# A causal convolution on TensorE: windows of 128 rows and 122 tokens against tiles of 64 rows and 58 tokens in the quarters of the array

## The chip, the cores and the metric

The kernel runs on one NeuronCore of one Trainium2 chip. The core has five engines with an instruction stream each: TensorE (PE in the profile; its weight loads are PEld), VectorE (DVE), ScalarE (ACT), GpSimd (POOL) and SyncE (SP, which here only issues DMAs). TensorE reads SBUF and writes PSUM; PSUM has eight banks of 512 float32 columns on 128 partitions. The metric is the device time of one execution in microseconds, the median over several runs. Each program is also profiled once; the profile gives the span from the first to the last instruction, start and duration of each instruction, and what ended the idle time before it.

## The reference, cut to what matters

```python
# x (8, 4224, 192); weight (8 heads, 7); moe_w_val, moe_w_out (192, 192); moe_conv_w (5, 192)
w = softmax(weight, axis=-1)                       # 7 taps for each of 8 heads
x_pad = concat([zeros(B, 6, D), x], axis=1)
x = sum_k w[h, k] * x_pad[:, s + k, h * 24 : h * 24 + 24]      # 24 channels to a head
gate_pre = sum_k conv_w[k] * pad(x, 4)[:, k : k + S, :]        # 5 taps, one weight per channel
gate = 1 / (1 + exp(-gate_pre))
out = (gate * (x @ w_val)) @ w_out
```

The first convolution has the same seven weights for all 24 channels of a head. The second has five weights per channel. Between them and the output lie two products with 192x192 matrices. All is float32.

## The kernel before, in words

**Tokens.** The eight sequences are laid end to end in two streams of four, so that each step handles two streams at once. Tokens are cut into 14 groups; `NJS` gives a group's size n (2, 3 or 5), and a group is cut into two or three steps by `BLOCKS` (304 and 302, twice 448, three times 502 tokens; the last group 500 and 188). There are 36 steps.

**First convolution (`conv_unit`, L304).** It runs on TensorE as a product with a band matrix. A window has 128 token rows (`WK`) and gives 122 tokens (`WIN`). For head h and window j the stationary operand is the input, 128 token rows by 120 columns (24 channels x 5 pieces of the group); the moving operand is `band`, 128 rows by 122 columns, which holds the softmaxed taps. The result lies channels by tokens. A unit is four windows in one PSUM bank, copied by ScalarE into `e` (L327); after a head's last window its rows go by DMA from `e` to the step layouts x1 and x2 (`scatter`, L339). The 192 channels are kept as 128 in x1 (both streams side by side, chunk a, index 0) and 64 + 64 in x2 (both streams stacked on partitions, chunk b, index 1).

**Second convolution.** It runs on ScalarE and VectorE. `gate_open` writes tap 0 into a PSUM accumulator (pa for chunk a, two banks; pb for chunk b, one bank), `gate_taps` adds taps 1 to 4 on VectorE (L397), `gate_close` takes the sigmoid on ScalarE (L410).

**Products.** Float32 values are split into a rounded float32r part h (cast on ScalarE, L418 and L426) and a rest l (subtraction on GpSimd, L419 and L427), and three products w.h*h + w.l*h + w.h*l are summed. v is the product with w_val, o the one with w_out. The 192x192 matrix is cut into blocks: `main` (128x128), `rows` (two row halves of 64), `diagonal` (128x128 with two blocks of 64), and `columns`, which stays in float32, cut into four pieces of the tokens and two column halves of the array. `gated` (L510) multiplies v by the sigmoid on VectorE, `split_gated1` and `split_gated2` split the result, `project` (L526) copies o out of PSUM and sends it.

**PSUM.** pa takes two banks, pb one; the other five are the pool `ps`, from which each of the six accumulators of a step (v2, v0, v1, o2, o0, o1; L433) and each unit of the convolution takes one bank.

**Order.** All engines run in the order in which the program is written (`manual_schedule`). Step n works on v of step n and o of step n-1; the convolution in it makes units of a group two groups ahead (`todo`, L547). Steps 0 to 3 are written out in a loop of their own (L580). From step 4 on the loop at L643 runs; there the taps of later steps are placed by `ahead`, `LEAD`, `BETWEEN`, `COST` and `FITS`: as many as a table of leads asks for, in the order all four of chunk a, all four of chunk b. `flush` closes a chunk whose taps are done and opens that chunk of the next step. On ScalarE, `flush(1)` stands behind `split_gated1` and in front of `project(n - 1, 0)`.

Of the kernel before, what the change touches and what calls it, by code (L numbers as in the profile page):

```python
# [7 lines left out]
F32 = mybir.dt.float32  # L8
# [10 lines left out]
HALO = KG - 1  # L19
WIN = 122  # L20
WK = WIN + KW - 1
NS = 5
# [7 lines left out]


NJS = [2, 3, 3, 3] + [5] * 8 + [3, 3]


def half(n):
    return (n * WIN - (KW - 1 if n % 2 else 0)) // 2


def reach(n):
    return 2 * n * WIN + half(n)  # L40
# [12 lines left out]


BLOCKS = {2: (304, 302), 3: (448, 448), 5: (502, 502, 502)}
for _n, _b in BLOCKS.items():
    assert sum(_b) == room(_n)
LEFT = TOTAL - sum(sum(BLOCKS[n]) for n in NJS[:-1])
# [17 lines left out]
LAST = N - 1  # L76
MB = 502
NMAX = max(NJS)
# [29 lines left out]
def kernel(  # L108
# [62 lines left out]
    w0 = cp.tile([128, NH, KW], F32, name="w0")  # L171
    band = cp.tile([WK, NH, WIN], F32, name="band")
    halves = [slice(4 * q, 4 * q + 4) for q in range(2)]
# [27 lines left out]
    nc.vector.memset(one, 1.0)  # L201
    zero = cp.tile([WK, M + WIN], F32, name="zero")
    nc.vector.memset(zero, 0.0)
# [3 lines left out]
    def zeros(k):  # L207
        pw = ps.tile([128, 512], F32, tag="p", name="pw")
        for i in range(k):
            nc.tensor.matmul(pw[:M, :WIN], lhsT=zero[:, :M], rhs=zero[:, M:], start=True, stop=True)  # L210
# [23 lines left out]
    for q in halves:  # L234
        nc.vector.tensor_tensor(out=band[:, q], in0=band[:, q], in1=wide(rs, WIN, q), op=ALU.mult)
    warm2 = cp.tile([128, 1], F32, name="warm2")
# [56 lines left out]


    x1s, x2s, es = {}, {}, {}
    units = []
    for g, n in enumerate(NJS):
        for q in range(2):
            ws = [(hi, j) for hi in range(4) for j in range(n)]
            for i in range(0, len(ws), 4):  # L300
                units.append((g, q, ws[i : i + 4]))
    first_unit = [next(i for i, u in enumerate(units) if u[0] == g) for g in range(NG)] + [len(units)]

    def conv_unit(u):  # L304
        g, q, ws = units[u]
        n = NJS[g]
        if u == first_unit[g]:
            x1s[g] = xp.tile([128, 2 * XB], F32, tag="x1", name=f"x1_{g}")
            x2s[g] = xp.tile([128, XC], F32, tag="x2", name=f"x2_{g}")
        if ws[0] == (0, 0):  # L310
            es[g, q] = ep.tile([M, 4 * NMAX * WIN], F32, tag="e", name=f"e_{g}_{q}")
        e = es[g, q]
        pc = ps.tile([128, 512], F32, tag="p", name=f"pc_{u}")
        for k, (hi, j) in enumerate(ws):
            h = QUADS[q][hi]
            i, at = home[g, h]
            c = (at * n + j) * M
            nc.tensor.matmul(  # L318
                pc[:M, k * WIN : (k + 1) * WIN],
                lhsT=xtiles[i][:, c : c + M],  # L320
                rhs=band[:, 4 * q + hi, :],
                start=True,
                stop=True,
            )
        a = (ws[0][0] * n + ws[0][1]) * WIN
        w = len(ws) * WIN
        nc.scalar.copy(e[:, a : a + w], pc[:M, :w])  # L327
# [64 lines left out]
    def gate_taps(n, i, k0=1, k1=KG):  # L392
        if n >= N:
            return
        acc = accs[n, i]
        for k in range(k0, k1):
            nc.vector.scalar_tensor_tensor(  # L397
                out=acc, in0=views(n, k)[i], scalar=cwt[:, i, k : k + 1],
                in1=acc, op0=ALU.mult, op1=ALU.add,
            )  # L400
# [21 lines left out]
    def split2(pool, tag, n, x):  # L422
# [5 lines left out]
        return h, l  # L428

    HALVES = (slice(0, 64), slice(64, 128))  # L430

# [14 lines left out]
    def diagonal(what, n):  # L446
        if not ok(n):
            return
        acc = bank(what, n, 2)
        w, _, _, h2, l2 = operands(what, n)  # L450
        r = slice(W22, W22 + 128)
        for i, (a, b) in enumerate(parts(w, h2, l2)):
            nc.tensor.matmul(acc, lhsT=a[:, r], rhs=b, start=(i == 0), stop=False)  # L453
# [26 lines left out]
    def columns(what, n):  # L480
        if not ok(n):
            return
        m = STEPS[n][2]
        acc = banks[what, n, 2]
        w = w_val if what == "v" else w_out
        x = views(n)[0] if what == "v" else g1s[n]
        cuts = [m * i // 4 for i in range(5)]
        for i in range(4):
            c = slice(cuts[i], cuts[i + 1])
            for q, p in enumerate(HALVES):  # L490
                nc.tensor.matmul(  # L491
                    acc[p, c], lhsT=w.f[:, W12 : W12 + 64], rhs=x[:, q, c],
                    start=False, stop=(i == 3),
                )
# [46 lines left out]
    def conv(k):  # L541
        for _ in range(k):
            if done[0] < len(units):
                conv_unit(done[0])
                done[0] += 1

    todo = [0] * (N + 1)  # L547
    for g in range(LAG, NG):
        a, b = SOON.get(g) or (first[g - LAG], first[g - 1])
        if g == NG - 1:  # L550
            a, b = a - 1, b - 1
        k = first_unit[g + 1] - first_unit[g]
        for i in range(k):
            todo[a + i * (b - a) // k] += 1
# [9 lines left out]
    zeros(WARM[1])  # L564
    conv(3)
    w_out.cast(nc.vector)
# [53 lines left out]
    T = KG - 1  # L620
    taps = [(n, i, k) for n in range(HEAD + 1, N) for i in range(2) for k in range(1, KG)]
    at_tap = [0]
    pending = []

    def flush(*which):
        for n, i in [p for p in pending if p[1] in which]:
            gate_close(n, i)
            gate_open(n + 1, i)
            pending.remove((n, i))

    def tap():
        n, i, k = taps[at_tap[0]]
        at_tap[0] += 1
        flush(*(j for m, j in pending if m < n and j == i))
        gate_taps(n, i, k, k + 1)
        if k == T:
            pending.append((n, i))

    def ahead(n):
        lead = LEAD[max(k for k in LEAD if k <= n)]  # L640
        return min(2 * T * (n - HEAD) + T + lead, len(taps))

    for n in range(HEAD, N + 1):  # L643
        diagonal("v", n)
        split(n + 1)
        diagonal("o", n - 1)
        main("v", n, 0)
        main("v", n, 1)
        while at_tap[0] < ahead(n):
            tap()  # L650
        columns("v", n)
        gated(n, 2)
        flush(0)
# [12 lines left out]
        used = first_used = 0  # L666
        while at_tap[0] < ahead(n + 1):
            _, i, k = taps[at_tap[0]]
            if used + COST[i] > FITS:
                break  # L670
            used += COST[i]
            tap()
            if (i, k) == (0, T):
                first_used = used
# [99 lines left out]
```

## Time and profile before

| | |
|---|---|
| median of 3 runs | 389.22 us (389.12 to 391.35) |
| the profiled execution | 387.03 us |
| its span, first to last instruction | 385.0 us |
| mean granted TensorE clock | 0.996 |
| TensorE idle in the span | 10.9 us |
| VectorE idle in the span | 43.0 us |
| moved by DMA | 82.49 MB |

The profile gives busy time by engine, by stretch of the span, and by group of equal instructions. A group's line gives source line, engine, operation, output and inputs with their shapes, how often, busy time, the mean duration of one in ns, and the engine's idle time before it with what ended it. Instructions of one engine overlap a little at their ends, so that durations add up to more than the time between starts. A float32 product appears as two weight loads and two matmuls, a float32r product as one of each. The chain of work that ended last is followed back from the last instruction; it shows which engine held the end at each time.

### The profile page before, as it was taken

To read this page: it belongs to the slowest core of one execution; us is meant where nothing else is said; L and a number is where in the kernel's file an instruction comes from. 1 tells how busy PE (TensorE), PEld (TensorE's weight loads), DVE (VectorE), ACT (ScalarE), POOL (GpSimd) and SP (SyncE) were. 2 spreads that over 40 slices of the span, in tenths; PEclk is the share of its full clock that TensorE was granted. 3 is DMA by queue.
4 is the path that set the end of the run, shared out by engine and by line. 5 is a ranking of instruction groups with operands and counts; after the bars stand their busy time and mean duration, and the time that the engine had idled before them with its cause. 6 is when DMAs were issued, how large, how long until landed. Compare 5 with 4: busy or idle time off the path is not lost.

```text
span 385.0 us, 8630 instructions
## 1 busy us (share of the span) xinstructions
PE 374.1 (97%) x3204; PEld 319.1 (83%) x3204; DVE 342.0 (89%) x428; ACT 327.3 (85%) x525; POOL 251.9 (65%) x173
## 2 busy tenths in 40 slices
PE   8899999999999999999999999999999999999895
PEld 8888887888888888888888888888888788887784
DVE  4899999789999999999999999899899988999970
ACT  7589888987999988898889988888888889987763
POOL 1869765656666667765765765677666775777771
PEclk9999999999999999999999999999999999999998
DMA  8899898999688688689777768868987645342224
GB/s 295 243 238 264 221 270 250 278 277 264 186 256 239 188 244 232 186 236 260 217 221 239 211 186 241 219 190 244 261 230 220 229 159 187 128 146 80 82 97 158
DMA packets 38209, 82.49 MB, mean 214 GB/s; under 512 B 4856, under 2 KB 17528, under 8 KB 38168
## 3 DMA queue, kind: packets, MB, share of 16 engines
q1 hardware_dynamic: 36720, 79.90, 69.5%
q0 software_dynamic: 896, 1.31, 1.5%
q10 hardware_dynamic: 552, 0.73, 0.6%
q8 instruction: 25, 0.41, 0.5%
q14 instruction: 16, 0.13, 0.1%
HBM read 29.34 MB, written 26.00 MB: 144 GB/s over the span
## 4 chain that ended last, share of the span: by engine, by line
PE 82%; DVE 6%; DMA 4%; ACT 4%; issue 1%; POOL 1%; SPq 1%; ACTq 0%; DVEq 0%; POOLq 0%
PE pc L318 20%; PE o L463 12%; PE v L463 11%; PE v L491 8%; PE v L476 7%; PE o L491 7%; PE o L476 6%; PE o L453 5%; PE v L453 5%; DVE pa L397 3%; DMA x<-e 2%; DVE g L510 2%; DMA x<-xw 1%; DVE pb L397 1%; DMA band<-bw 1%
## 5 line engine op out<-in xcount | busy, mean ns | idle before, releaser
L397 DVE SCALAR_TENSOR_TENSOR pa<-x,cwt,pa 128x1004 f32<-128x1004 f32 (+5 forms) x144 | 172.8, 1200 | 4.6 <-ACT pa L390 0.9
L419 POOL TENSOR_TENSOR xl<-x,xh 128x1004 fp32r<-128x1004 f32 (+5 forms) x36 | 74.8, 2078 | 80.1 <-ACT xh L418 70.4
L397 DVE SCALAR_TENSOR_TENSOR pb<-x,cwt,pb 128x502 f32<-128x502 f32 (+5 forms) x144 | 102.2, 710 | 3.9 <-ACT pb L390 0.7
L318 PEld LDWEIGHTS pc<-band,x 128*120 128x120 f32 x912 | 101.1, 184 | 3.9 <-issue 1.6
L318 PE MATMUL pc<-band,x 128*120 128x122 f32 x912 | 102.1, 269 | 1.3 <-DMA x<-xw 1.3
L419 POOL TENSOR_TENSOR pl<-g,ph 128x1004 fp32r<-128x1004 f32 (+5 forms) x36 | 79.1, 2198 | 21.1 <-ACT ph L418 19.5
L510 DVE TENSOR_TENSOR g<-v,g 128x502 f32<-128x502 f32 (+5 forms) x108 | 65.9, 642 | 20.7 <-PE v L476 16.5
L327 ACT COPY e<-pc 120x488 f32<-120x488 f32 x114 | 61.3, 577 | 7.9 <-PE pc L318 6.7
L526 ACT COPY ot<-o 128x502 f32<-128x502 f32 (+5 forms) x108 | 55.8, 549 | 3.1 <-PE o L463 2.6
L427 POOL TENSOR_TENSOR pl<-g,ph 128x502 fp32r<-128x502 f32 (+5 forms) x36 | 43.4, 1206 | 13.3 <-ACT ph L426 13.0
L418 ACT CAST ph<-g 128x1004 fp32r<-128x1004 f32 (+5 forms) x36 | 35.3, 980 | 14.6 <-DVE g L510 14.5
L410 ACT ACTIVATE g<-pa 128x1004 f32<-128x1004 f32 (+5 forms) x36 | 34.7, 964 | 12.2 <-DVE pa L397 12.1
L427 POOL TENSOR_TENSOR xl<-x,xh 128x502 fp32r<-128x502 f32 (+5 forms) x36 | 41.8, 1161 | 3.3 <-ACT xh L426 3.2
L390 ACT ACTIVATE pa<-x,cwt 128x1004 f32<-128x1004 f32 (+5 forms) x36 | 37.8, 1050 | 1.9 <-DMA x<-xw 0.5
L491 PEld LDWEIGHTS v<-x,wvf 128*64 128x64 f32 x576 | 29.1, 136 | 11.8 <-issue 11.2
L491 PE MATMUL v<-x,wvf 128*64 128x125 f32 (+4 forms) x576 | 37.2, 270 | 0.0
L491 PE MATMUL o<-g,wof 128*64 128x125 f32 (+4 forms) x576 | 35.5, 264 | 0.0
L418 ACT CAST xh<-x 128x1004 fp32r<-128x1004 f32 (+5 forms) x36 | 35.2, 978 | 0.0
L491 PEld LDWEIGHTS o<-g,wof 128*64 128x64 f32 x576 | 30.9, 136 | 0.1
L463 PE MATMUL o<-ph,woh 128*128 128x502 f32 (+5 forms) x72 | 30.8, 428 | 0.0
L463 PE MATMUL v<-xl,wvh 128*128 128x502 f32 (+5 forms) x72 | 27.2, 378 | 0.5 <-POOL xl L419 0.5
L463 PE MATMUL v<-xh,wvh 128*128 128x502 f32 (+5 forms) x72 | 27.3, 379 | 0.3 <-ACT e L327 0.3
(75 smaller groups left out, 565.0 us busy)
## 6 DMA issues: line engine op xcount, KB each, us to landing
x<-xw SPq DMA_DIRECT2D x64, 300.0 KB
out<-ot SPq DMA_DIRECT2D x24, 753.0 KB
x<-e SPq DMA_DIRECT2D x40, 285.9 KB
x<-xw SPq DMA_DIRECT2D x20, 360.0 KB
out<-ot SPq DMA_DIRECT2D x8, 672.0 KB
x<-e SPq DMA_DIRECT2D x32, 141.6 KB
x<-e SPq DMA_DIRECT2D x25, 171.6 KB
x<-e SPq DMA_DIRECT2D x16, 94.4 KB
```

The costliest lines, as they stand in the source:

```text
L318: nc.tensor.matmul(pc[:M, k * WIN : (k + 1) * WIN], lhsT=xtiles[i][:, c : c + M], rhs=band[:, 4 * q + hi, :], start=True, stop=True,)
L327: nc.scalar.copy(e[:, a : a + w], pc[:M, :w])
L397: nc.vector.scalar_tensor_tensor(out=acc, in0=views(n, k)[i], scalar=cwt[:, i, k : k + 1], in1=acc, op0=ALU.mult, op1=ALU.add,)
L418: nc.scalar.copy(h, x)
L419: nc.gpsimd.tensor_tensor(out=l, in0=x, in1=h.bitcast(F32), op=ALU.subtract)
L427: nc.gpsimd.tensor_tensor(out=l, in0=x, in1=h.bitcast(F32), op=ALU.subtract)
L453: nc.tensor.matmul(acc, lhsT=a[:, r], rhs=b, start=(i == 0), stop=False)
L463: nc.tensor.matmul(acc, lhsT=a[:, r], rhs=b[:, q], start=(fresh and i == 0), stop=(not fresh and i == 2))
L476: nc.tensor.matmul(acc, lhsT=a[p, r], rhs=b[p], start=(fresh and i == 0), stop=(not fresh and i == 2))
L491: nc.tensor.matmul(acc[p, c], lhsT=w.f[:, W12 : W12 + 64], rhs=x[:, q, c], start=False, stop=(i == 3),)
L510: nc.vector.tensor_tensor(out=v, in0=banks.pop(("v", n, q)), in1=v, op=ALU.mult)
L526: nc.scalar.copy(ots[n][:, q * m : (q + 1) * m], banks.pop(("o", n, q)))
```

## The change

- A window becomes two tiles of 64 token rows (`HK`) that give 58 tokens each (`HW`), so a window gives 116 tokens. The stationary operand is 64 rows by 64 or 56 columns, the moving operand 64 rows by 58 columns. Each of the four combinations of row half and column half is a product in one quarter of the array; the two row halves write to two PSUM banks. A unit takes 4, 6 or 7 windows (`UNIT`), two banks of `ps`, and two copies on ScalarE, which put the two halves of each window side by side in `e`.
- Block sizes follow: 288 twice, 432 twice, 482 three times; one group of 3 becomes one of 5. There are 59 windows for each head instead of 57, and 37 steps instead of 36; the last group has 500 and 244 tokens.
- From step 4 on the taps follow a fixed pattern: two of chunk a at the start of a step, one of chunk b behind `gated(n, 2)`, one of chunk b between `gated(n, 0)` and `gated(n, 1)`, then a, b, a, b. The tables of leads go. `flush(1)` moves to the start of the step, and all units of a step stand at its end.
- Before the first step two units instead of three stand between the two warm-up stretches of zero products, and the last group's units are no longer made a step earlier. The layout of the inputs on the host follows the tiles.

```diff
+HK = 64
+HW = HK - KW + 1
+WIN, WK = 2 * HW, 2 * HK
+ZW = 122
-NJS = [2, 3, 3, 3] + [5] * 8 + [3, 3]
+NJS = [2, 3, 3, 3] + [5] * 9 + [3]
-BLOCKS = {2: (304, 302), 3: (448, 448), 5: (502, 502, 502)}
+BLOCKS = {2: (288, 288), 3: (432, 432), 5: (482, 482, 482)}
+UNIT = {2: 4, 3: 6, 5: 7}
-LEAD = {0: 0, 10: 1, 13: 2, 16: 3, 19: 4, 28: 3, 30: 2, 32: 1, 33: 0}
-BETWEEN = {9, 12, 15, 18}
-COST, FITS = (1.3, 0.78), 4.6
...
-        pc = ps.tile([128, 512], F32, tag="p", name=f"pc_{u}")
+        pc = [ps.tile([128, 512], F32, tag="p", name=f"pc_{u}_{r}") for r in range(2)]
         for k, (hi, j) in enumerate(ws):
             h = QUADS[q][hi]
             i, at = home[g, h]
             c = (at * n + j) * M
-            nc.tensor.matmul(
-                pc[:M, k * WIN : (k + 1) * WIN],
-                lhsT=xtiles[i][:, c : c + M],
-                rhs=band[:, 4 * q + hi, :],
-                start=True,
-                stop=True,
-            )
-        a = (ws[0][0] * n + ws[0][1]) * WIN
-        w = len(ws) * WIN
-        nc.scalar.copy(e[:, a : a + w], pc[:M, :w])
+            for r, c0, c1 in ((0, 0, 64), (1, 64, M), (0, 64, M), (1, 0, 64)):
+                p = HALVES[r]
+                nc.tensor.matmul(
+                    pc[r][c0:c1, k * HW : (k + 1) * HW],
+                    lhsT=xtiles[i][p, c + c0 : c + c1],
+                    rhs=band[p, 4 * q + hi, :],
+                    start=True,
+                    stop=True,
+                )
+        a = ws[0][0] * n + ws[0][1]
+        w = len(ws)
+        ev = e[:, : 4 * n * WIN].rearrange("p (w r t) -> p w r t", r=2, t=HW)
+        for r in range(2):
+            nc.scalar.copy(ev[:, a : a + w, r, :], pc[r][:M, : w * HW].rearrange("p (w t) -> p w t", t=HW))
...
+    def taps(order):
+        for c in order:
+            i = "AB".index(c)
+            n, k = HEAD + 1 + at_tap[i] // T, 1 + at_tap[i] % T
+            if n < N:
+                gate_taps(n, i, k, k + 1)
+                at_tap[i] += 1
+                if k == T:
+                    pending.append((n, i))
...
+    taps("AA")
     for n in range(HEAD, N + 1):
         diagonal("v", n)
+        flush(1)
         split(n + 1)
         diagonal("o", n - 1)
         main("v", n, 0)
         main("v", n, 1)
-        while at_tap[0] < ahead(n):
-            tap()
+        taps("AA")
         columns("v", n)
         gated(n, 2)
         flush(0)
+        taps("B")
         columns("o", n - 1)
         split_gated2(n)
         project(n - 1, 2)
         rows("v", n)
-        if n in BETWEEN:
-            tap()
         gated(n, 0)
+        taps("B")
         gated(n, 1)
         rows("o", n - 1)
         split_gated1(n)
-        flush(1)
         main("o", n - 1, 0)
...
+        taps("ABAB")
         project(n - 1, 0)
         main("o", n - 1, 1)
         project(n - 1, 1)
-        now = min(todo[n], 2 if first_used else 0)
-        conv(now)
-        flush(0)
-        conv(todo[n] - now)
-        flush(1)
+        conv(todo[n])
```

More of the change, by code (lines that the diff above doesn't have):

```diff
@@ L52, in room @@
     return min(reach(n), NS * fifth(n)) - HALO
-BLOCKS = {2: (304, 302), 3: (448, 448), 5: (502, 502, 502)}
+BLOCKS = {2: (288, 288), 3: (432, 432), 5: (482, 482, 482)}
 for _n, _b in BLOCKS.items():
-    assert sum(_b) == room(_n)
+    assert sum(_b) <= room(_n)
 LEFT = TOTAL - sum(sum(BLOCKS[n]) for n in NJS[:-1])
@@ L76 @@
 LAST = N - 1
-MB = 502
+MB = 500
 NMAX = max(NJS)
@@ L171 @@
     w0 = cp.tile([128, NH, KW], F32, name="w0")
-    band = cp.tile([WK, NH, WIN], F32, name="band")
+    band = cp.tile([WK, NH, HW], F32, name="band")
     halves = [slice(4 * q, 4 * q + 4) for q in range(2)]
@@ L209, in zeros @@
         for i in range(k):
-            nc.tensor.matmul(pw[:M, :WIN], lhsT=zero[:, :M], rhs=zero[:, M:], start=True, stop=True)
+            nc.tensor.matmul(pw[:M, :ZW], lhsT=zero[:, :M], rhs=zero[:, M:], start=True, stop=True)
     zeros(WARM[0])
@@ L234 @@
     for q in halves:
-        nc.vector.tensor_tensor(out=band[:, q], in0=band[:, q], in1=wide(rs, WIN, q), op=ALU.mult)
+        nc.vector.tensor_tensor(out=band[:, q], in0=band[:, q], in1=wide(rs, HW, q), op=ALU.mult)
     warm2 = cp.tile([128, 1], F32, name="warm2")
@@ L291 @@
     w_val, w_out = Weight("wv"), Weight("wo")
+    HALVES = (slice(0, 64), slice(64, 128))
     x1s, x2s, es = {}, {}, {}
@@ L299 @@
             ws = [(hi, j) for hi in range(4) for j in range(n)]
-            for i in range(0, len(ws), 4):
-                units.append((g, q, ws[i : i + 4]))
+            for i in range(0, len(ws), UNIT[n]):
+                units.append((g, q, ws[i : i + UNIT[n]]))
     first_unit = [next(i for i, u in enumerate(units) if u[0] == g) for g in range(NG)] + [len(units)]
@@ L564 @@
     zeros(WARM[1])
-    conv(3)
+    conv(2)
     w_out.cast(nc.vector)
@@ L620, with flush @@
     T = KG - 1
-    taps = [(n, i, k) for n in range(HEAD + 1, N) for i in range(2) for k in range(1, KG)]
-    at_tap = [0]
+    at_tap = [0, 0]
     pending = []
-    def flush(*which):
-        for n, i in [p for p in pending if p[1] in which]:
+    def taps(order):
[7 more added lines that the diff above has]
+                    pending.append((n, i))
+    def flush(i):
+        for n, _ in [p for p in pending if p[1] == i]:
             gate_close(n, i)
@@ L629, in flush @@
             pending.remove((n, i))
[L631 to L641, printed above, removed]
+    taps("AA")
     for n in range(HEAD, N + 1):
         diagonal("v", n)
+        flush(1)
         split(n + 1)
@@ L663 @@
         split_gated1(n)
-        flush(1)
         main("o", n - 1, 0)
[L666 to L674, printed above, removed]
+        taps("ABAB")
         project(n - 1, 0)
@@ L697 @@
     for g, n in enumerate(NJS):
-        w2 = WK // 2
         c = 5 * HC
-        win = np.empty((NS * n, WK, D), f)
+        win = np.empty((NS * n, 2, HK, D), f)
         for w in range(NS * n):
-            q = w * WIN
-            if q + WIN <= reach(n):
-                win[w, :, :c] = flat[0, base + q : base + q + WK, :c]
-            elif q >= second(n):
-                q += base - second(n)
-                win[w, :, :c] = flat[1, q : q + WK, :c]
-            else:
-                win[w, :w2, :c] = flat[0, base + q : base + q + w2, :c]
-                win[w, w2:, :c] = flat[1, base : base + w2, :c]
-            r, j = divmod(w, n)
-            q = base + r * fifth(n) + j * WIN
-            if 2 * j + 2 <= n:
-                win[w, :, c:] = flat[0, q : q + WK, c:]
-            elif 2 * j >= n:
-                q += fifth(n) - n * WIN
-                win[w, :, c:] = flat[1, q : q + WK, c:]
-            else:
-                win[w, :w2, c:] = flat[0, q : q + w2, c:]
-                q = base + r * fifth(n)
-                win[w, w2:, c:] = flat[1, q : q + w2, c:]
+            for i in range(2):
+                t, q = divmod(w * WIN + i * HW, second(n))
+                win[w, i, :, :c] = flat[t, base + q : base + q + HK, :c]
+                r, q = divmod(w * WIN + i * HW, n * WIN)
+                t, q = divmod(q, half(n))
+                q += base + r * fifth(n)
+                win[w, i, :, c:] = flat[t, q : q + HK, c:]
         base += TOKS[g]
-        win = win[:, ::-1].reshape(NS, n, WK, NH, HC)
+        win = win[:, :, ::-1].reshape(NS, n, WK, NH, HC)
         for i in range(0, NH, PER_LOAD[n]):
@@ L729 @@
     taps = weight[order, ::-1]
-    bw = np.full((WK, NH, WIN), -1e30, f)
-    for p in range(WK):
-        for i in range(max(0, WIN - 1 - p), min(WIN, WIN - 1 - p + KW)):
-            bw[p, :, i] = taps[:, p + i - (WIN - 1)]
+    bw = np.full((2, HK, NH, HW), -1e30, f)
+    for p in range(HK):
+        for i in range(max(0, HW - 1 - p), min(HW, HW - 1 - p + KW)):
+            bw[:, p, :, i] = taps[:, p + i - (HW - 1)]
     def packed(w):
```

13 lines of the change are left out of this document (4 added, 9 removed).

## The prediction

> **What bounds the kernel now.** I read the page first (busy time of each engine, the chain), then the windows by stage, then the chain in order of time, and one step of the timeline.
>
> ```profile
> span 385.0 us, 8630 instructions
> PE 374.1 (97%) x3204; PEld 319.1 (83%) x3204; DVE 342.0 (89%) x428; ACT 327.3 (85%) x525; POOL 251.9 (65%) x173
> ...
> PE pc L318 20%; PE o L463 12%; PE v L463 11%; PE v L491 8%; PE v L476 7%; PE o L491 7%; PE o L476 6%; PE o L453 5%; PE v L453 5%; DVE pa L397 3%; DMA x<-e 2%; DVE g L510 2%; DMA x<-xw 1%; DVE pb L397 1%; DMA band<-bw 1%
> ```
>
> TensorE sets the time, and the convolution (L318) is its largest piece. But VectorE is only 32 us behind, and ScalarE 47 us: this bounds what any saving on TensorE can bring.
>
> ```profile
> core 0: us, PE busy (x) PEld busy (x) DVE busy (x) ACT busy (x) POOL busy (x), PEclk, DMA share, GB/s
> 26.00:54.00 28.00, 27.05 (x264) 23.82 (x264) 25.60 (x35) 24.66 (x44) 22.82 (x21) 1.00 0.88 251
> 108.00:278.00 170.00, 170.00 (x1428) 143.62 (x1427) 158.10 (x181) 151.19 (x233) 111.64 (x66) 1.00 0.79 227
> ```
>
> In the long middle TensorE never idles, VectorE is at 93%, ScalarE at 89%. The period comes from the chain: its `PE o L463` pieces are the second projection's main products, one per step.
>
> ```profile
> 52.76 1.42 PE o L463 x6
> 106.45 1.42 PE o L463 x6
> 117.42 1.56 PE o L463 x6
> 276.09 1.56 PE o L463 x6
> 363.92 1.43 PE o L463 x6
> ```
>
> From 117.42 to 276.09 are 15 steps of 502 tokens: 10.58 us a step, 21.1 ns a token.
>
> **The change, part by part.** *Convolution.* Today each window costs two passes of 128x122.
>
> ```profile
> 245.72 2.68 PE L318 MATMUL pc<-band,x 128*120 128x122 f32 x24
> 248.16 0.47 PE L453 MATMUL v<-xh,wvh 128*128 128x502 f32 x1
> ...
> 250.75 0.39 PE L463 MATMUL v<-xl,wvh 128*128 128x502 f32 x1
> ...
> 251.07 1.08 PE L491 MATMUL v<-x,wvf 128*64 128x125 f32 x16
> 251.98 1.03 PE L491 MATMUL o<-g,wof 128*64 128x125 f32 x16
> ...
> 253.50 0.39 PE L476 MATMUL v<-xl,wvh 64*128 64x502 f32 x2
> 253.73 0.45 PE L476 MATMUL o<-ph,woh 64*128 64x502 f32 x2
> 253.99 1.27 DVE L510 TENSOR_TENSOR g<-v,g 128x502 f32<-128x502 f32 x2 [0.36 <-PE v L476]
> ...
> 255.18 1.26 DVE L397 SCALAR_TENSOR_TENSOR pa<-x,cwt,pa 128x1004 f32<-128x1004 f32 x1
> 255.30 1.03 ACT L418 CAST ph<-g 128x1004 fp32r<-128x1004 f32 x1 [0.54 <-DVE g L510]
> ```
>
> 24 passes from 245.72 to 248.16 are 0.102 us each, and a float32 product takes two, so 0.20 us a window; 456 windows are 93 us. The new window needs eight passes of 58 columns, two in each quarter of the array. No row shows quarters. The nearest are L491, two column halves at a time, and among them the last step, whose 47 columns are the narrowest:
>
> ```profile
> 374.27 0.67 PE L491 MATMUL v<-x,wvf 128*64 128x47 f32 x16
> 374.76 1.06 PE L491 MATMUL o<-g,wof 128*64 128x125 f32 x16
> ```
>
> 16 passes in 0.49 us are 0.061 us for each pair of halves that run together. At 125 columns a pair takes 0.91/8 = 0.114 us, so at 47 it is no longer the columns that count but the weight load of 64. L476 shows two row halves side by side as well: 253.50 to 253.73 is 0.23 us for two of 502, what one whole pass takes. If rows and columns overlap together, four quarters cost 0.06 us, a window 0.12 us. That is the low end. The high end is the rate at which instructions reach the array:
>
> ```profile
> L491 PEldq EVENT_SEMAPHORE  x3: 51/51/51, 21.8 to 22.0; - x3
> L318 PEldq EVENT_SEMAPHORE  x1: 51/51/51, 22.6 to 22.6; - x1
> ...
> 22.53 0.75 PE L491 MATMUL v<-x,wvf 128*64 128x76 f32 x16
> 23.21 0.41 PE L476 MATMUL v<-xh,wvh 64*128 64x304 f32 x2
> ```
>
> Between the semaphore at 22.0 and the one at 22.6 TensorE's sequencer took in all that stands between them in the program: 44 instructions (16 weight loads and 16 products of L491, 6 and 6 of L476), while the first of them only began at 22.53. That is 0.55 us or a little more, at most some 0.0125 us each. Sixteen of a window would be 0.20 us, as dear as today. If only two quarters ran at a time it would be 0.24. I take 0.12, the value nearest to the 47-column row: the 0.0125 is an upper bound, and the queue fills while long products execute.
>
> Against it stands a rule. The Trainium skill ("TensorEngine Tiling (Array Packing)", Instruction Overhead) advises against taking a tiling factor from a dimension that is already small, for about 60 cycles of overhead per matmul; 58 columns are such a dimension. "TensorE: Matmul & The Clock Gate" (Wait — 56ns, not 53.3ns?) puts a floor of about 25 ns on starts, by which eight passes would be an estimated 0.20 us and the sum an estimated 400 us instead of the 384 below. The 47-column row, 0.031 us a pass, lies above that floor and doesn't test it.
>
> Windows rise to 472 (8 heads x 59). A step of 482 tokens then has 13.3 windows, 1.6 us, where 13.3 of the old kind took 2.7. Added are two changes of array shape, into quarters and out, in each step with convolution. A like change: the last L463 pass begins at 250.75 and streams 0.23, the first L491 begins at 251.07, 0.09 later; and a first pass takes 0.47 where a later one takes 0.39. That is 0.17 us a change; I take 0.15 in and 0.25 out, bounds 0 and 0.7 together. TensorE without waits: from 248.16 (first L453) to 253.73 (end of the v rows) 5.57 us, at 482 tokens 5.35; then o rows 0.65, change 0.25, main o 1.3, change 0.15, conv 1.6, change 0.25: 9.55 us.
>
> *Taps in alternation.* A tap that reads what the one before wrote waits for its end.
>
> ```profile
> 298.61 1.28 DVE pa L397
> 299.92 1.28 DVE pa L397
> ...
> L397 DVE SCALAR_TENSOR_TENSOR pa<-x,cwt,pa 128x1004 f32<-128x1004 f32 x96 | 121.6, 1267 | 2.5
> L397 DVE SCALAR_TENSOR_TENSOR pb<-x,cwt,pb 128x502 f32<-128x502 f32 x96 | 71.3, 743 | 2.7 <-ACT pb L390 0.7
> L510 DVE TENSOR_TENSOR g<-v,g 128x502 f32<-128x502 f32 x72 | 46.6, 676 | 12.1 <-PE v L476 11.7 <-PE v L491 0.2
> ```
>
> Taps on one accumulator start 1.31 us apart; the two products at 253.99 start 0.60 apart though each takes 0.676. So an alternating order saves some 0.08 us from one instruction to the next. At 482 tokens (slopes of about 1.05 ns an element from the 448 and 502 forms): 8 taps and 3 products, ten of eleven overlapping, are 9.0 us instead of 9.5. VectorE is no longer the bound.
>
> *Copies out of PSUM.* ten copies of 488 columns per three steps become twelve of 348 or 406.
>
> ```profile
> L327 ACT COPY e<-pc 120x488 f32<-120x488 f32 x114 | 61.3, 577 | 7.9 <-PE pc L318 6.7
> L526 ACT COPY ot<-o 128x502 f32<-128x502 f32 x72 | 38.9, 574 | 0.0
> L526 ACT COPY ot<-o 128x188 f32<-128x188 f32 x3 | 0.9, 316 | 1.1 <-PE o L463 0.7 <-PE o L491 0.3
> L418 ACT CAST ph<-g 128x1004 fp32r<-128x1004 f32 x24 | 24.8, 1032 | 12.6 <-DVE g L510 12.5
> ```
>
> From 188 to 502 columns a copy grows 0.82 ns a column: 406 take 0.51 us, four a step 1.9, what 3.3 copies of 488 cost before. All ScalarE work of a step is 0.889 x 10.58 = 9.4 us now; at 482 tokens without the copies 7.3, with them 9.2. The sigmoid of chunk b and the multiplication that opens the next one (0.6 and 0.7 us) move from behind `ph` to the head of the next step, ahead of the casts of x: those come 1.3 us later, and GpSimd's subtraction behind them too, but their products are due a whole step later. No DMA issue changes its place in SyncE's or GpSimd's queue.
>
> *The new wait.* A unit now takes two of the five PSUM banks of `ps`. When the units of a step begin, two banks hold o0 and o1, three are free or soon free. The first unit takes two, the second one and a bank that `project(n-1, 0)` must empty. That copy stands on ScalarE behind the cast `ph` of `split_gated1`, which needs `gated(n, 1)`, now behind a B tap. From the end of the v rows: 0.26 to the first product (253.73 to 253.99), product 0.58, tap 0.64, product 0.65, to the cast 0.04 (253.99 + 1.27 to 255.30), cast 0.92 net, copy 0.56, release 0.05: 3.7 us. TensorE could be there after 0.65 + 0.25 + 1.3 + 0.15 + 0.8 = 3.15. So the second unit waits 0.55 us, and behind it the next step's products. Period: 3.7 + second unit 0.8 + change 0.25 + 5.35 = 10.1 us for 482 tokens, 21.0 ns a token: in the middle nearly all of the gain is lost.
>
> *Start.*
>
> ```profile
> L227 ACT ACTIVATE band<-band,nmx 128x122 f32<-128x122 f32 x8 | 2.5, 384 | 0.0
> ```
>
> Eight exponentials of the band over 58 columns instead of 122 save 8 x 64 x 0.82 ns = 0.4 us ahead of the first copies, and these, in smaller pieces, let the first transfers go as much earlier: -0.8. Then VectorE, 91% busy from 26 to 54, has steps 3% shorter: -1.2. Together -2.0 (bounds 0 and -4).
>
> *Tokens and transfers.* One step more (37), 3.5% more input bytes; the DMA share of 0.79 to 0.88 covers it, SyncE issues 92 loads for 88. Uncovered, 3.5% of 0.8 of the middle would be 5 us.
>
> **Sum**, against the profiled span of 385.0. Until 52.76: -2.0. From 52.76 to 106.45 (5 steps, 53.7 us, with five units of the old kind in two of them): new steps of 432 tokens by the same loop are 3.45 + 0.8 + 0.25 + 4.9 = 9.4 us; in the two with three units the third waits for the copies of the first, one us more. So 3 x 9.4 + 2 x 10.35 = 48.9, -4.8. To 363.92, 257.5 us for 25 steps: now 22 with two units, 10.1 each, and 4 with one or none, 9.0 each on VectorE: 258.2, +0.7. The end: +0.5 for a last step of 244 instead of 188. Total -5.6: span 379.4. The profiled execution took 387.0, 2.0 more than its span, so 381.4; the median of runs is 2.2 above the profiled one: 383.6.
>
> **Rivals.** (1) Slower: the quarters are fed, not computed. At 0.20 us a window the second unit (6.7 windows) grows by 0.53 us, 22 steps by 11.7, the steps with three units and with one by 5: 400 us. For it: the 0.0125 above. Against: it is a bound only. It decides from where the 5.6 us are eaten: 0.08 x 5.6 / 16.7 above 0.12, some 0.147 us a window. 0.20.
> (2) The bank wait doesn't show, TensorE runs its 9.55 us: 22 x 0.55 = 12 less, 371 us. Against: five banks and the fixed order on ScalarE. 0.16.
> (3) No change: with three engines within 10% of the period, small waits add 0.25 us a step: 5.5 more, 389 us. For: the 11.7 us that L510 already waits for L476. 0.17.
>
> **How the numbers follow.** The forecast, 0.47, covers 379 to 388 (the loop good to 0.2 us a step). About 1% (3.9 us) is what a measurement can tell from no change. Faster: three quarters of the forecast and (2), 0.52. Same: the rest and most of (3), 0.28. Slower: (1), 0.20. Range 371 to 398, from (2) to most of (1).
>
> **What would show it.** Right: 0.12 us a window in L318's rows; TensorE waiting about 0.5 us a step in conv for ScalarE's L526; taps 0.08 us closer; period 10.1. Wrong: windows above 0.15 us, no wait before the second unit, or ScalarE without idle time.

## The result, and the profile after

| | before | after |
|---|---|---|
| median of six runs | 389.17 us | 384.64 us |
| the profiled execution | 387.03 us | 383.81 us |
| its span | 385.0 us | 382.0 us |
| TensorE idle in the span | 10.9 us | 25.5 us |

The changed kernel takes 0.988 of the time before (95% interval 0.985 to 0.991): 1.2% faster. Five of its runs lie between 381.89 and 385.46; one of 641.69 was disturbed and is left out of the ratio. 383.6 was predicted. The sum came out, in part by luck: the terms for the early steps and for the long middle were off by 3.6 and 3.0 us, in opposite directions.

The page of the changed kernel: busy time, the chain's shares, the convolution's group.

```profile
span 382.0 us, 14551 instructions
PE 356.5 (93%) x6130; PEld 289.1 (76%) x6130; DVE 331.7 (87%) x439; ACT 327.6 (86%) x570; POOL 251.1 (66%) x177
...
PE 43%; DVE 14%; ACT 13%; DMA 12%; POOL 9%; issue 5%; SPq 3%; DVEq 0%; ACTq 0%; POOLq 0%
...
L319 PE MATMUL pc<-band,x 64*56 64x58 f32 (+1 forms) x3776 | 74.4, 220 | 14.7 <-ACT ot L527 9.1
```

In the kernel before, the chain's shares were these:

```profile
PE 82%; DVE 6%; DMA 4%; ACT 4%; issue 1%; POOL 1%; SPq 1%; ACTq 0%; DVEq 0%; POOLq 0%
```

TensorE was busy 97% of the span and held 82% of the chain. Now it is busy 93% and holds 43%, and the chain passes from engine to engine: none is full, each waits for another. The row of L319 says where: 9.1 of the convolution's 14.7 idle microseconds ended when ScalarE had copied `ot` out of PSUM (L527, `project`).

One such step, first the row of TensorE that begins the o rows (the v rows end there), then the chain of waits from that step on.

```profile
203.77 0.38 PE L477 MATMUL o<-ph,woh 64*128 64x482 f32 x2
```

```profile
204.61 0.72 DVE pb L400
205.33 0.57 DVE g L511
205.90 0.02 issue
205.92 1.00 ACT ph L421
206.92 0.47 ACT ot L527
207.39 0.04 issue
207.43 1.03 PE pc L319 x50
208.47 0.86 PE v L454 x3
```

This is the wait that was predicted, link by link: the B tap, the second gated product, the cast `ph`, the copy of o0, and then the second unit, 3.66 us behind the end of the v rows (3.7 predicted). The marks by which the steps were counted before, the first main product of o, in the changed kernel:

```profile
52.12 0.47 PE L464 MATMUL o<-ph,woh 128*128 128x432 f32 x1
...
104.58 0.46 PE L464 MATMUL o<-ph,woh 128*128 128x432 f32 x1
114.60 0.48 PE L464 MATMUL o<-ph,woh 128*128 128x482 f32 x1
...
294.42 0.48 PE L464 MATMUL o<-ph,woh 128*128 128x482 f32 x1
...
359.76 0.49 PE L464 MATMUL o<-ph,woh 128*128 128x482 f32 x1
```

From 114.60 to 294.42 are 18 steps of 482 tokens: 9.99 us a step.

### The profile page after: what moved, and what is told of

It reads as the page before. It is cut to its first block, busy times and chain, and to the rows that moved or that the text cites. A ratio compares the mean times of both kernels' runs of the same rounds, so it can differ in the third digit from the quotient of the medians.

```text
span 382.0 us, 14551 instructions
## 1 busy us (share of the span) xinstructions
PE 356.5 (93%) x6130; PEld 289.1 (76%) x6130; DVE 331.7 (87%) x439; ACT 327.6 (86%) x570; POOL 251.1 (66%) x177
## 4 chain that ended last, share of the span: by engine, by line
PE 43%; DVE 14%; ACT 13%; DMA 12%; POOL 9%; issue 5%; SPq 3%; DVEq 0%; ACTq 0%; POOLq 0%
DMA x<-e 11%; PE v L464 8%; DVE g L511 6%; PE pc L319 6%; ACT ph L421 6%; PE v L492 6%; PE v L477 5%; PE o L492 5%; DVE pb L400 5%; PE v L454 5%; PE o L454 4%; POOL pl L422 4%; ACT ot L527 3%; PE o L464 2%; SPq L359 2%
## 5 line engine op out<-in xcount | busy, mean ns | idle before, releaser
L400 DVE SCALAR_TENSOR_TENSOR pa<-x,cwt,pa 128x964 f32<-128x964 f32 (+4 forms) x148 | 173.2, 1170 | 2.3 <-ACT pa L393 0.4
L422 POOL TENSOR_TENSOR xl<-x,xh 128x964 fp32r<-128x964 f32 (+4 forms) x37 | 73.5, 1987 | 81.5 <-ACT xh L421 70.5
L400 DVE SCALAR_TENSOR_TENSOR pb<-x,cwt,pb 128x482 f32<-128x482 f32 (+4 forms) x148 | 102.4, 692 | 0.6
L422 POOL TENSOR_TENSOR pl<-g,ph 128x964 fp32r<-128x964 f32 (+4 forms) x37 | 79.6, 2152 | 29.1 <-ACT ph L421 25.1
L511 DVE TENSOR_TENSOR g<-v,g 128x482 f32<-128x482 f32 (+4 forms) x111 | 69.5, 631 | 32.8 <-PE v L492 20.0
L319 PE MATMUL pc<-band,x 64*56 64x58 f32 (+1 forms) x3776 | 74.4, 220 | 14.7 <-ACT ot L527 9.1
L319 PEld LDWEIGHTS pc<-band,x 64*56 64x56 f32 (+1 forms) x3776 | 65.3, 132 | 28.1 <-ACT ot L527 13.5
L330 ACT COPY e<-pc 120x348 f32<-120x348 f32 (+2 forms) x148 | 59.5, 489 | 5.1 <-PE pc L319 5.1
L527 ACT COPY ot<-o 128x482 f32<-128x482 f32 (+4 forms) x111 | 56.2, 538 | 3.0 <-PE o L464 2.4
L430 POOL TENSOR_TENSOR pl<-g,ph 128x482 fp32r<-128x482 f32 (+4 forms) x37 | 43.6, 1179 | 2.7 <-ACT ph L429 2.7
```

Source lines behind the costliest of these rows:

```text
L319: nc.tensor.matmul(pc[r][c0:c1, k * HW : (k + 1) * HW], lhsT=xtiles[i][p, c + c0 : c + c1], rhs=band[p, 4 * q + hi, :], start=True, stop=True,
L330: nc.scalar.copy(ev[:, a : a + w, r, :], pc[r][:M, : w * HW].rearrange("p (w t) -> p w t", t=HW))
L400: nc.vector.scalar_tensor_tensor(out=acc, in0=views(n, k)[i], scalar=cwt[:, i, k : k + 1], in1=acc, op0=ALU.mult, op1=ALU.add,)
L422: nc.gpsimd.tensor_tensor(out=l, in0=x, in1=h.bitcast(F32), op=ALU.subtract)
L430: nc.gpsimd.tensor_tensor(out=l, in0=x, in1=h.bitcast(F32), op=ALU.subtract)
L511: nc.vector.tensor_tensor(out=v, in0=banks.pop(("v", n, q)), in1=v, op=ALU.mult)
```

## The experiments

Each was timed beside the kernel before (388.6 to 389.0 us in these sessions). A period is the mean over the same 18 steps.

| kernel | median, us | ratio to before (95%) | period, us |
|---|---|---|---|
| the changed kernel | 384.64 | 0.988 (0.985 to 0.991) | 9.99 |
| project_first | 370.64 | 0.955 (0.949 to 0.962) | 9.36 |
| tap_behind | 374.90 | 0.964 (0.959 to 0.969) | 9.53 |
| row_halves | 403.13 | 1.037 (1.031 to 1.043) | 10.64 |
| quarter_order | 369.87 | 0.952 (0.947 to 0.957) | 9.36 |
| before_new_taps | 388.10 | 0.998 (0.995 to 1.001) | (502 tokens) |
| after_old_taps | 392.12 | 1.006 (1.003 to 1.010) | 9.75, later 10.6 |
| old_taps_project_first | 391.51 | 1.007 (1.003 to 1.010) | 10.05 |
| old_taps_flush_moved | 385.63 | 0.988 (0.984 to 0.992) | 9.93 |
| fewer_zeros | 376.55 | 0.968 (0.963 to 0.974) | 9.57 |
| head_order | 372.16 | 0.958 (0.952 to 0.964) | 9.38 |
| spread_units | 450.07 | 1.149 (1.139 to 1.160) | 9.33 and 18 |
| four_two | 368.64 | 0.950 (0.946 to 0.954) | 9.36 |

### The wait for o0's bank: project_first, tap_behind

project_first moves one call on ScalarE:

```diff
         rows("o", n - 1)
-        split_gated1(n)
         main("o", n - 1, 0)
+        project(n - 1, 0)
+        split_gated1(n)
         taps("ABAB")
-        project(n - 1, 0)
         main("o", n - 1, 1)
```

> The changed kernel with one call moved: project(n-1, 0), the copy that empties o0's bank, stands ahead of split_gated1 on ScalarE instead of behind it. Theory (the second unit of a step waits for that bank because the copy stands behind the cast ph, which waits for the second gated product): the wait of 0.4 to 0.5 us in front of the second unit goes, the period falls from 9.99 us to about 9.55, and over some 22 steps the time falls by 8 to 11 us, to 374 to 377. Rival 1 (the wait is not that bank's, or another wait as late takes its place): no change, 383 to 386. Rival 2 (ScalarE has no room: the earlier copy makes ph and what hangs on it later): 385 or more.

Measured: 370.64 us, a larger gain than expected. The same place of the step in its timeline, and the window of the middle (busy time of TensorE, its weight loads, VectorE, ScalarE, GpSimd):

```profile
198.80 1.02 ACT L527 COPY ot<-o 128x482 f32<-128x482 f32 x2
198.95 0.65 DVE L511 TENSOR_TENSOR g<-v,g 128x482 f32<-128x482 f32 x1
...
199.42 0.38 PE L464 MATMUL o<-pl,woh 128*128 128x482 f32 x1
199.71 1.00 ACT L421 CAST ph<-g 128x964 fp32r<-128x964 f32 x1
199.74 1.74 PE L319 MATMUL pc<-band,x 64*64 64x58 f32 x104
...
201.41 0.48 PE L454 MATMUL v<-xh,wvh 128*128 128x482 f32 x1
```

```profile
108.00:278.00 170.00, 170.00 (x3044) 137.75 (x3045) 162.99 (x201) 162.01 (x275) 121.75 (x73) 1.00 0.87 251
```

The copy now stands ahead of `ph`, both units run in one piece of 104 products, and TensorE has no idle time in 170 us. A step takes 9.36 us, 0.63 less than 9.99; over the 26 steps of the long middle the marks show 241.1 us for 255.2, and the three early steps with two units had the same wait (0.2 to 1.1 us). I had expected 0.45 a step in 22 steps. In the changed kernel the wait is 0.68 by starts: 50 products from 206.02 at 0.0146 each end at 206.75, the next starts at 207.43. The profile's idle column shows less of it (0.39), because it counts a product as busy for 0.22 us, although one is let in every 15 ns.

tap_behind leaves ScalarE alone and takes the B tap out of the chain:

```diff
         gated(n, 0)
-        taps("B")
         gated(n, 1)
+        taps("B")
```

> The changed kernel with one tap moved: the tap of chunk b between gated(n, 0) and gated(n, 1) stands behind gated(n, 1). Nothing is moved on ScalarE or TensorE. Theory (that tap, some 0.6 us, stands in the chain v rows, g0, tap, g1, ph, copy of o0, second unit): the chain gets 0.5 us shorter by the starts in the trace (g0 at 204.03, g1 at 205.23), the wait in front of the second unit nearly goes, the period falls from 9.99 to 9.4 to 9.5, the time to 371 to 376. Rival (ScalarE or VectorE is the bound there, the chain is not): 382 to 386.

Measured: 374.90 us, a period of 9.53. Two ways to shorten the same chain, on two engines: the first takes the wait away, the second all but 0.17 us a step of it. That it is the chain, and not an engine's load, is shown.

### What makes a window cheap: row_halves, quarter_order

row_halves is the changed kernel with the columns left whole:

```diff
-            for r, c0, c1 in ((0, 0, 64), (1, 64, M), (0, 64, M), (1, 0, 64)):
+            for r, c0, c1 in ((0, 0, M), (1, 0, M)):
```

> The changed kernel with the columns left whole: each window is two tiles of 64 rows by 120 columns, side by side, instead of four of 64 by 64 or 56. Same products, same outputs, half the instructions. Theory (a set of tiles takes as long as its widest weight load, so that the halved load is what makes a window cheap): 0.20 us a window instead of 0.117, the second unit grows by 0.55 us, and the time goes to 396 to 402. Rival (it is the 58 streamed columns that count, the split of the columns does nothing): 0.12 us a window, 383 to 386. If the number of instructions were the limit, half of them would make it faster: below 382.

Measured: 403.13 us, a little over the range, with half of the convolution's instructions. Its two units, in TensorE's timeline:

```profile
205.26 3.15 PE L319 MATMUL pc<-band,x 64*120 64x58 f32 x56
208.34 0.49 PE L454 MATMUL v<-xh,wvh 128*128 128x482 f32 x1
```

56 products are 14 windows; less the 0.27 that the last one is shown to take, 0.206 us a window. In project_first 104 products are 13 windows: (1.74 - 0.22) / 13 = 0.117. The streamed columns are the same 58; what differs is the weight load, 120 columns against 64. The starts of the single products in the traces settle it. The two row halves start 0.007 us apart, so they do run side by side, and the next two follow 0.105 behind the first. The products of the old window, with the same load of 120 columns and 122 streamed ones, start 0.105 apart as well. So the load sets the pace of such narrow products; to stream half as many columns gains nothing by itself.

quarter_order is project_first with the quarters in another order:

```diff
-            for r, c0, c1 in ((0, 0, 64), (1, 64, M), (0, 64, M), (1, 0, 64)):
+            for r, c0, c1 in ((0, 0, 64), (0, 64, M), (1, 0, 64), (1, 64, M)):
```

> project_first with the four quarters of a window in another order: both column halves of the upper rows first, then both of the lower rows; before, the order went crosswise. Theory (four tiles run at once and the set takes what its weight loads take): the same 0.117 us a window, the same time, 369 to 372. Rival (only tiles without a common row group or column group run side by side, so that the crosswise order is needed): up to 0.23 us a window, 395 or more.

Measured: 369.87 us, the same period. The order in which the four quarters are fed makes no difference.

### The taps: before_new_taps, after_old_taps and two more

before_new_taps is the kernel before with the new loop, after_old_taps the changed kernel with the old one (its tables, `tap`, `flush` and loop, word for word).

> The kernel before with the new order of taps alone (alternating taps, a B tap between the gated products, all units at the end of a step); windows of 128x122 and block sizes as before. Theory (TensorE sets the time there; what VectorE saves is off the path): no change, 387 to 392. Rival (part of the gain is the taps'): 380 to 386.

> The changed kernel with the tap order of before (table of leads, all four taps of chunk a, then all four of b, units split by flush). Theory: the gated products stand together again in most steps, so the chain from the v rows to the copy of o0 is 0.6 us shorter and the wait for the bank goes; but VectorE, at 9.5 us a step with taps that wait for one another, becomes the bound at 9.6 to 10 us: 375 to 384, at most the same as the changed kernel. Rival (the alternation is needed for the gain): 388 or more.

Measured: 388.10, no difference from before; and 392.12, 0.6% slower than before. The first is as expected. In the second my theory failed, and the rival's number came. ScalarE and TensorE in one step of after_old_taps:

```profile
301.79 1.00 ACT L424 CAST ph<-g 128x964 fp32r<-128x964 f32 x1 [1.12 <-DVE g L514]
...
302.69 0.57 ACT L416 ACTIVATE g<-pb 128x482 f32<-128x482 f32 x1
303.30 0.67 ACT L396 ACTIVATE pb<-x,cwt 128x482 f32<-128x482 f32 x1
303.90 1.01 ACT L530 COPY ot<-o 128x482 f32<-128x482 f32 x2
304.50 0.28 PE L322 MATMUL pc<-band,x 64*56 64x58 f32 x4 [0.97 <-ACT ot L530]
```

In the old loop `flush(1)` stands between `ph` and the copy of o0: sigmoid and multiplication of chunk b, 1.2 us more in front of the bank. The chain has lost the tap, but the flush has come into it. Two further kernels took this apart. old_taps_project_first:

```diff
         rows("o", n - 1)
-        split_gated1(n)
-        flush(1)
         main("o", n - 1, 0)
+        project(n - 1, 0)
+        split_gated1(n)
...
-        project(n - 1, 0)
         main("o", n - 1, 1)
         project(n - 1, 1)
+        flush(1)
```

> The changed kernel with the tap order of before, as in after_old_taps, but with project(n-1, 0) ahead of split_gated1 and the closing and opening of chunk b behind project(n-1, 1), so that no unit waits for o0's bank. Tells whether the old order of taps was dear because of what it put on ScalarE in front of that copy, or because its taps keep VectorE longer. Theory (the place of the copy is what counts; VectorE with taps that wait for one another needs 9.5 us a step against TensorE's 9.33): a period of 9.5 to 9.7 us, 373 to 379. Rival (the alternation itself is needed: gated products late behind four taps in a row): above 384.

Measured: 391.51 us, above the rival's bound. But the reason is not VectorE alone. The flush now stands ahead of the copies of the units, TensorE waits for these at the next `diagonal` (0.39 us at 304.77), and ScalarE's share of the chain is 24%:

```profile
PE 56%; ACT 24%; DVE 10%; DMA 4%; issue 3%; SPq 1%; POOL 0%; ACTq 0%; DVEq 0%
```

So in old_taps_flush_moved the flush of chunk b went where the changed kernel has it, behind `diagonal("v", n)` of the next step. The order on VectorE and the closing of chunk a that hangs on it are left of the old scheme.

> old_taps_project_first with one more move: closing and opening chunk b (flush of chunk b) stands behind diagonal v of the next step, as in the changed kernel, and not ahead of the copies of the units. What is left of the old tap order is then the order on VectorE alone: four taps of chunk a in a row, four of chunk b in a row. Theory (what made the two kernels with the old taps slow is where that flush stands on ScalarE; VectorE's order is worth only the 0.08 us per transition): period at most 9.6 us, 370 to 378. Rival (taps in blocks delay the gated products or the sigmoids by themselves): above 384, with TensorE or ScalarE waiting for VectorE.

Measured: 385.63 us, a period of 9.93 (10.1 in its last ten steps). VectorE and TensorE in one step:

```profile
238.46 3.01 DVE L403 SCALAR_TENSOR_TENSOR pb<-x,cwt,pb 128x482 f32<-128x482 f32 x4 [0.44 <-ACT pb L396]
241.38 1.79 DVE L514 TENSOR_TENSOR g<-v,g 128x482 f32<-128x482 f32 x3
...
242.08 0.48 PE L480 MATMUL o<-ph,woh 64*128 64x482 f32 x1 [0.26 <-DVE g L514]
243.08 5.00 DVE L403 SCALAR_TENSOR_TENSOR pa<-x,cwt,pa 128x964 f32<-128x964 f32 x4
```

VectorE is the bound here. From 238.46 to 243.08 it takes 4.6 for four B taps and three products, then 5.0 for four A taps, and 0.44 until chunk b is open: with taps in blocks nothing else is there to do meanwhile. The rival holds: once TensorE no longer waits for banks, the order of the taps, with the closings and openings that hang on it, is worth 15 us (385.63 against 370.64), while in the kernel before it is worth nothing.

### The early steps and a wait that has no releaser: fewer_zeros, head_order, spread_units, four_two

In step 4 of the changed kernel TensorE stood still in front of one product with its weights long loaded:

```profile
70.10 0.21 PE L319 MATMUL pc<-band,x 64*64 64x58 f32 x1 [1.50 <-issue]
```

It waits on no semaphore. fewer_zeros, on project_first, moves all later instructions 56 places ahead in TensorE's stream:

```diff
-ZW = 122
+ZW = 244
-WARM = 11, 5, 14
+WARM = 6, 3, 7
```

> project_first with the warming zero products 244 columns wide and half as many (16 for 30), so that TensorE's instruction stream is 56 instructions shorter ahead of the first step, for the same time. In both traces one product at instruction 2756 of TensorE's stream, with no semaphore to wait for, starts 1.4 to 1.5 us late, and one at 1477, 1279 or 5 x 256 less one earlier, 0.5 late. Theory (instructions come in blocks of 256 = 16 KB, and 256 instructions of the quarters run off in some 2 us, faster than the next block comes): the edge of the block moves 56 instructions on, into the products of the next step, and this wait of 1.4 us goes: 368 to 370.5 against 370.6, and the stalls, if any, are at other products, again multiples of 256 apart. Rival (the wait belongs to that product, through data or a PSUM bank): it stays at the same product, with 1.4 us.

(The second position meant is 1477.) Measured: 376.55 us; the time is a miss, the place is not. The wait at that product is gone, and new ones stand elsewhere; one is again at position 1477, where another product stands now. Among the new ones:

```profile
25.82 0.47 PE L319 MATMUL pc<-band,x 64*56 64x58 f32 x5 [4.95 <-issue]
...
197.71 0.33 PE L319 MATMUL pc<-band,x 64*56 64x58 f32 x4 [2.30 <-issue]
```

Counted in the compiled programs, these are instructions 708 and 7108 of TensorE's stream; the one at 70.10 is number 2756. All leave 196 when divided by 256. The last section has the whole count.

head_order, on project_first, changes ScalarE's order at the end of step 3 (`n == HEAD - 1`):

```diff
         gate_taps(n + 1, 0, k, KG)
+        conv(todo[n] - now)
         gate_close(n + 1, 0)
         gate_open(n + 2, 0)
         gate_taps(n + 1, 1)
-        conv(todo[n] - now)
```

> project_first with the last unit of step 3 written ahead of the closing and opening of chunk a, so that on ScalarE the copies of the third unit stand in front of the sigmoid and not behind it. Theory (TensorE's 1.4 to 1.7 us of waiting at the head of step 4 for a copy L330 is due to that sigmoid and multiplication, 2 us on ScalarE, ahead of it): the wait goes or falls below 0.4, the step from 54 to 66 takes about 10.7 instead of 12.0 us, and the time falls by about 1 us, to 369 to 370. Rival (VectorE, 95% busy in that stretch, sets its length): no change in the length of that step.

Measured: 372.16 us, nothing gained. The copies came earlier and TensorE's wait at `diagonal` went, but the opening of chunk a, now behind them, came later, and with it VectorE:

```profile
60.37 4.60 DVE L400 SCALAR_TENSOR_TENSOR pa<-x,cwt,pa 128x864 f32<-128x864 f32 x4 [1.95 <-ACT pa L393]
...
65.54 0.46 PE L477 MATMUL o<-ph,woh 64*128 64x432 f32 x1 [3.41 <-DVE g L511]
```

That step took 13.5 us instead of 12.0. VectorE sets its length, as the rival says.

spread_units, on project_first:

```diff
-SOON = {2: (0, 2), 3: (1, 3), 4: (3, 5), 5: (5, 8)}
+SOON = {2: (0, 2), 3: (1, 3), 4: (3, 6), 5: (6, 9)}
-        a, b = SOON.get(g) or (first[g - LAG], first[g - 1])
+        a, b = SOON.get(g) or (first[g - LAG] + 1, first[g - 1] + 1)
```

> project_first with the units of the convolution spread out: groups 4 and 5 take three steps each (3 to 8) with two units a step, where steps 3 and 4 had three, and all later groups move one step back. Theory (steps 3 and 4 take 12.0 and 11.7 us because the third unit waits for copies, and 288 instructions of the quarters run off faster than the next block of 256 comes): both become 10 to 10.5 us, the product at instruction 2756 is no longer at a block's edge inside three units, one step near the end gets 0.6 us longer: 367 to 369.5 against 370.6. Rival (VectorE, 95% busy in these steps, sets their length): no change, 370 to 372.

Measured: 450.07 us. Every third step takes 17 to 19 us, because a new group's chunk a is opened before its transfers have landed, and ScalarE with all that stands behind it waits:

```profile
89.57 1.07 ACT L393 ACTIVATE pa<-x,cwt 128x964 f32<-128x964 f32 x1 [8.14 <-DMA x<-e]
...
91.57 0.70 PE L319 MATMUL pc<-band,x 64*64 64x58 f32 x16 [7.87 <-ACT ot L527]
```

The convolution's lead of one whole step is needed for its transfers; neither theory had this. But the early steps say what was asked: step 3 took 11.96 us with two units as with three, step 4 took 8.82 instead of 11.65. four_two, on project_first, uses that:

```diff
+    todo[3], todo[4] = todo[3] + 1, todo[4] - 1
```

> project_first with one unit of group 4 moved from step 4 to step 3: four and two units there instead of three and three, everything else as before it; the group is complete at the end of step 4 as before. In spread_units step 4, with two units, took 8.8 us instead of 11.7, and step 3 took 12.0 us with two units as with three, so that VectorE sets its length. Theory (in step 4 the third unit and the edge of an instruction block are what cost; in step 3 there is room beside VectorE's taps): step 4 takes 8.8 to 9.5 us, step 3 at most 1 us more than 12.0, the time falls by 1.5 to 2.5 us to 368 to 369. Rival (step 3 pays for the fourth unit what step 4 saves, in waits for banks or for another block of instructions): 370 to 372.

Measured: 368.64 us. Steps 3 and 4 take 12.75 and 8.84 us, together 2.0 less than in project_first, as expected; the medians differ by 2.0 too, though their intervals overlap. Of the 2.8 us that step 4 gains, 1.42 are the wait of project_first at instruction 2756, which does not come here; no run tells whether all of the other 1.4 is the third unit's. It is the fastest kernel here: 5.0% below the kernel before.

## Why the prediction was right, and where it was not

- **Price of a window**: 0.12 predicted, 0.117 measured. The 47-column row was the right neighbour. The bound of 0.0125 us an instruction was only a bound: 16 instructions run in 0.117, 0.0073 each. The price that rival 1 feared exists, though for the weight load and not for the feeding of instructions: row_halves has it (0.206), and takes 403 us where 400 was worked out.
- **Where the skill spoke against it**: the Trainium skill ("TensorEngine Tiling (Array Packing)", Instruction Overhead) warns of the overhead of each matmul when a small dimension is split. The traces do not agree for tiles that run side by side: splitting the columns doubled the instructions and cut the time of a window from 0.206 to 0.117 us. Eight products start 0.0146 us apart on average, so the estimate of 0.20 us a window that stood against the forecast did not come.
- **Array shapes**: 0.4 us a step for two changes predicted. In project_first the first product of the convolution comes 0.32 after the last main pass, 0.10 more than the usual 0.22; 13 windows later it is 201.26, and the next `diagonal` starts at 201.41, 0.15 later; its first product holds up the second for 0.32 (201.41 to 201.73), again 0.10 more than usual: 0.35 together.
- **TensorE without waits**: 9.55 predicted, 9.36 measured; **VectorE**: 9.0 predicted, 153.5 us in 17.0 steps of the middle of the changed kernel, also 9.0. Its 9.5 without alternation is 9.6 in old_taps_flush_moved (4.6 + 5.0), before the 0.44 of waiting.
- **The new wait**: mechanism and place right, 0.55 predicted, 0.68 by starts. TensorE was there earlier than I thought (2.98 us behind the end of the v rows, 3.15 predicted), the copy when I thought. Period 10.1 predicted, 9.99 measured. Rival 2's 371 us, the time without this wait, is what project_first takes; but it gained 14.0 us and not 12, from a time that was 1.0 higher.
- **The terms that failed**, against the prediction's sum, by the marks:

| stretch | before | predicted change | measured change |
|---|---|---|---|
| to the mark at 52 | 52.76 | -2.0 | -0.6 |
| five steps | 53.69 | -4.8 | -1.2 |
| the long middle | 257.47 (25 steps) | +0.7 | -2.3 (255.18, 26 steps) |
| the end | 21.1 | +0.5 | +1.2 |
| span | 385.0 | -5.6 | -3.0 |

  *Five steps* is the step of the working that was wrong. It took steps of TensorE's length, 9.4 us and one more for a third unit. Step 3 is VectorE's (95% busy, 11.4 of 12.0 us) and took 11.96, as spread_units shows with two units as with three. Step 4 took 11.73 for its third unit and 1.5 us of an instruction block. In step 6 o0's bank was 0.86 late, where 9.4 had left no room for the wait; ScalarE had itself stood 1.68 us for a transfer (`x<-e`) ahead of that copy. The row of before was there to be read: VectorE was busy 25.60 of the 28 us just ahead of these steps.
  *The start*: ScalarE's first copy did come 0.4 earlier (7.40 against 7.80), but VectorE's first tap did not (17.89 against 17.81): the last of the transfers between them was issued at 12.28 against 12.05 and had landed at 16.96 against 16.78. More cannot be said; in the kernels here that share this code the mark of step 3 lies anywhere from 52.1 to 55.5.
  *The middle* was better than predicted by 22 steps of 0.1 and by steps without units that took 8.9 us.
- **The median**: 2.2 us were added for the runs' median over the profiled execution. In the six runs of the changed kernel it is 0.8. So that term was 1.4 too large, and the gain in the span 2.6 too large. That the two nearly cancel is luck, and it is why 383.6 came out so near to 384.64.

## What to carry to other kernels

When a stage is made cheaper by giving it more of a shared resource (here two PSUM banks a unit instead of one), walk the chain that frees that resource, across all engines, and compare it with the shortened stage: this one cost two thirds of a microsecond a step, most of what could be gained, and moving a single copy on ScalarE ahead of a cast gave it back. An order of instructions that is worth nothing behind a full engine can be worth much when that engine is no longer full, so test it again in the new kernel. And judge each stretch by the engine that bounds it there: step 3 was VectorE's, and cheaper products could not shorten it.

## What the hardware did that I had not expected

**Instructions can run out.** The queue that fetches instructions moved twice as much in the changed kernel (0.41 MB in 25 packets before):

```profile
q8 instruction: 48, 0.79, 0.9%
```

That is 16 KB a packet, 256 instructions of 64 bytes. In the eleven kernels with quarter tiles, 29 products start more than 0.3 us late without any semaphore to wait for, by 0.32 to 4.95 us. All 29 stand at position 196 or 197 of a block of 256 in TensorE's stream, and of the 256 instructions in front of each at least 188 belong to quarter tiles:

| instruction (mod 256) | kernels, wait in us |
|---|---|
| 452 (196) | old_taps_project_first 1.23, four_two 0.65, quarter_order 0.58, old_taps_flush_moved 0.54, tap_behind 0.42 |
| 708 (196) | fewer_zeros 4.95 |
| 964 (196) | after_old_taps 1.64, head_order 1.36, tap_behind 1.00 |
| 1477 (197) | the changed kernel 0.32, and six others up to 1.35 |
| 2244 (196) | old_taps_flush_moved 1.24, fewer_zeros 0.83 |
| 2756 (196) | the changed kernel 1.50, project_first 1.42, tap_behind 2.73, and five others |
| 7108 and 9156 (196), 10949 (197) | fewer_zeros 2.30 and 0.89, after_old_taps 0.48 |

The kernel before, before_new_taps and row_halves, with half as many instructions in a window or fewer, have none. A window's 16 instructions run in 0.117 us, so 256 last 1.9 us inside the convolution; in the changed kernel a packet of 16 KB was on its way for 0.9 to 1.9 us, and around its two waits (30 to 40 and 66 to 72 us) the DMA engines were 87% and 81% busy. The packets' times in the traces show what ended the waits. If the first packet is taken for the third block of 256, the packet of the block that begins at the late product had landed 1.2 to 1.7 us before that product started, in all 29; in the three kernels without such waits every packet had landed 5.4 us or more before its block began. These waits sum to 1.8 us in the changed kernel, 10.2 in fewer_zeros and nothing in spread_units. The Trainium skill ("Runtime: NRT & Kernel Launch", Instruction fetch mechanics) states such blocks of 16 KiB; it also states that crossing one is mostly hidden, and that holds here behind longer products (none of these waits in those three kernels) and not behind a block of quarter tiles. Two of the 29 late products are themselves longer ones (9156 in `diagonal`, 10949 in `columns`). Why a packet comes late at one edge and not at another is left open: no kernel was run with the transfers taken away.

**Four tiles cost one weight load.** Four quarter tiles, eight products and eight weight loads, run in 0.117 us whatever their order. That is 0.058 for each set of four, as much as the two column halves of L491 in the kernel before take by their starts with 47 streamed columns and loads of 64 (0.058). Two half tiles with loads of 120 columns take 0.206 a window.
